# Summing the softmax exponentials of three or four query groups at once on GpSimd

## The chip, the core and the metric

The kernel runs on one core of a Trainium2 chip. The metric is the device time of one execution in microseconds; the kernel before was timed three times and its median is 1094.3 us (1091.17 to 1095.49). The profile shown below is of one more execution.

The core has four compute engines that run their own instruction streams and meet at semaphores: TensorE (PE, matmuls; PEld is its loading of weights), VectorE (DVE), ScalarE (ACT) and GpSimd (POOL). SyncE (SP) issues the transfers.

## The reference

For each of 4 batches there are 12,480 queries, keys and values of width 128, and 49 agents. All arithmetic is in float32.

```python
a2k = softmax(scale * agents @ k.T)          # 49 x 12480
agent_v = a2k @ v                            # 49 x 128
q2a = softmax(scale * q @ agents.T)          # 12480 x 49
x = q2a @ agent_v                            # 12480 x 128, all batches: 49920 rows
h = x @ w_in                                 # 49920 x 2048
out = (h * cos(h)) @ w_out                   # 49920 x 128
```

Each softmax is `e = exp(s - max)`, divided by `e.sum() + 1e-09`. The change touches how the sums `e.sum()` of `q2a` are formed: for each query, 49 exponentials are added up.

## The kernel before

**Tiling.** The queries are worked in groups of 960, 13 groups to a batch, 52 in all. A group stands in SBUF as 8 tiles (`GT`) of 120 queries; some groups are laid out on 126 partitions (`QT`), so that the exponentials `e` of one group are a 126 x 8 x 49 block. A group takes 16 steps (`STEP`); the main loop runs through 832 steps and 4 more. In a step n, TensorE makes `ph`, two 128 x 480 blocks of h (`first_product`, L1119, from the weights `a` and the turned query weights `pT`), ScalarE takes the cosine (`c`, L1122), VectorE forms `r = (cos - 1) * h` (`cubic_part`, L1128), and TensorE multiplies the `r` of step n - 4 by `w_out` (`second_product`, L1144; L1140 and L1141 add the linear part). `ph` and the small blocks called `one` lie in PSUM, all other names in SBUF. There are 3 buffers of `ph`, 6 of `r` and 3 of `pT`.

**What a query group needs before its 16 steps.** Scores `q @ agents` (L169, L177), their maximum (VectorE, `mx`, L734), the subtraction (GpSimd, `e<-e,mx`, L736 and L782), the exponential (ScalarE, L791), the sum (`query_sum`, L796 to L808), 1/sum (VectorE, `query_inverse`, L810 to L814), the product of both (GpSimd, `query_weights`, `p<-e,rz`, L819), transposes on TensorE (L833), a copy out of PSUM on ScalarE (L838) and the split into `pT` on GpSimd (L843, L844).

**Bursts and pieces.** The exponential and the sine need different tables in ScalarE, so the exponentials are collected: in each batch, at its step 97 (`BURST`), one burst takes the exponentials of a piece of 7 query groups (A), of the next batch's keys (K) and of a piece of 6 query groups (B), each as one instruction. In the last batch there is only one piece, of 5 groups. The earliest five groups have a burst of their own in which VectorE forms the sums (`vector_sum`); the first three groups, in the opening, are summed one by one on GpSimd.

**A sum on GpSimd.** `query_sum` adds up one group (8 x 49 numbers in each partition) with seven additions: 24 + 24 columns, 12 + 12, 6 + 6, 3 + 3 (all into the tile `tree`, L802), then the three left and the 49th column into `rz` (L804, L805, L806). Behind the last group of a piece one more instruction adds `EPS` to the sums of the whole piece (L808). For the opening's groups and the early piece VectorE adds `EPS` (L813).

**What sets the order.** A plan maps steps to calls. `burst` plans the seven sums of piece A at steps +1, +1, +3, +3, +9, +11 and +13 behind the burst and those of piece B at +16, +18 and so on; 1/sum of A stands at +16, of B at +42. `query_weights` of group n stands 10 steps ahead of the group, its transposes 7 ahead (or the next free place). Every engine then works its list in order. `kept_behind` ties the GpSimd instructions of a call to the one traced ahead of them, so that the sums keep their place among GpSimd's other work.

Of the kernel before, what the change touches and what calls it, by code (L numbers as in the profile page):

```python
# [9 lines left out]
F32 = mybir.dt.float32  # L10
# [8 lines left out]
P = 128  # L19
# [4 lines left out]
GT = 8  # L24
# [4 lines left out]
EPS = 1e-9  # L29
# [17 lines left out]
def agent_attention_cos_ffn(ctx, tc, qT, kT, v, vk, vk_rest, agT, w_in, w_out, outT):  # L47
    nc = tc.nc
# [70 lines left out]
    @contextmanager  # L119
    def kept_behind(engines):  # L120

        traced = nc.cur_bb.bb.instructions
        start = len(traced)
        last = {}
        for i in reversed(traced):
            if i.engine in engines and i.engine not in last:
                last[i.engine] = i
            if len(last) == len(engines):
                break
        yield  # L130
        for i in list(traced[start:]):
            if i.engine in engines:
                tc.add_manual_dep(i, last[i.engine].name, mybir.DependencyInfo(mybir.DependencyClass.NoSync,
                                  mybir.DependencyReason.DATA), reason="kept_behind")
                last[i.engine] = i
# [281 lines left out]
    class First(Fast):  # L417
# [87 lines left out]
        def summed(self):  # L505
            sums = self.sb.tile([KR, P], F32, name="sums", bufs=1)
            nc.vector.tensor_copy(sums, self.po)
            yield
            pv = self.psum()[:, :KR]
            nc.tensor.matmul(pv, sums, fold, start=True, stop=True)  # L510
            yield
            nc.vector.tensor_copy(self.av, pv)
            yield
# [159 lines left out]
    with ExitStack() as pools:  # L673
        sb = pools.enter_context(tc.tile_pool(name="sb", bufs=2))
# [26 lines left out]
        PER = NG * STEP  # L701
        NQ = NB * NG
        NSTEP = NB * PER
        e_of, rz_of, closes = {}, {}, {}
        PIECES = 7

        def piece_tiles(piece):
            e = sb.tile([QT, PIECES * GT, NA], F32, name="e", bufs=3)
            rz = sb.tile([QT, PIECES * GT], F32, name="rz2", bufs=4)
            for i, k in enumerate(piece):  # L710
                e_of[k], rz_of[k] = e[:, i * GT:(i + 1) * GT], rz[:, i * GT:(i + 1) * GT]
                e_of[piece], rz_of[piece] = e[:, :len(piece) * GT], rz[:, :len(piece) * GT]
            if piece != early:
                closes[piece[-1]] = piece

        def query_parts(n, piece, wide=False, by_vector=False):
            b, g = n // NG, n % NG
            src = qT[b, :, g * GRP:(g + 1) * GRP + (QT - TT if n in plain else 0)]
            if wide:
                ps = scores_twice(sb.tile([P, 2 * 512], F32, name="xt", bufs=3)[:, :GRP], src, b, pair())  # L720
                yield
            else:
                ps = query_scores(sb, src, b, small(), n in plain).rearrange("p (h t) a -> p h t a", h=2)
                yield
            if n == piece[0]:
                piece_tiles(piece)
            e = e_of[n].rearrange("p (h t) a -> p h t a", h=2)
            if not wide:
                (nc.vector.tensor_copy if by_vector else nc.scalar.copy)(e, ps)
                ps = e  # L730
                yield
            mx = sb.tile([QT, GT], F32, name="mx2", bufs=6)
            mx = mx.rearrange("p (h t) -> p h t", h=2)
            nc.vector.reduce_max(mx, ps, axis=AX.X)  # L734
            on = nc.vector if wide else nc.gpsimd
            on.tensor_sub(e, ps, mx.unsqueeze(3).to_broadcast([QT, 2, HT, NA]))  # L736
# [56 lines left out]
        def vector_sum(n):  # L793
            nc.vector.reduce_sum(rz_of[n], e_of[n], axis=AX.X)

        def query_sum(n):  # L796

            e, rz = e_of[n], rz_of[n].unsqueeze(2)
            t = sb.tile([e.shape[0], GT, 24], F32, name="tree", bufs=1)
            src, w = e, 24  # L800
            while w > 2:
                nc.gpsimd.tensor_add(t[:, :, :w], src[:, :, :w], src[:, :, w:2 * w])  # L802
                src, w = t, w // 2
            nc.gpsimd.tensor_add(rz, t[:, :, 0:1], t[:, :, 1:2])  # L804
            nc.gpsimd.tensor_add(rz, rz, t[:, :, 2:3])  # L805
            nc.gpsimd.tensor_add(rz, rz, e[:, :, 48:49])  # L806
            if n in closes:
                nc.gpsimd.tensor_scalar_add(rz_of[closes[n]], rz_of[closes[n]], EPS)  # L808

        def query_inverse(piece):  # L810
            rz = rz_of[piece]
            if piece not in closes.values():
                nc.vector.tensor_scalar_add(rz, rz, EPS)  # L813
            nc.vector.reciprocal(rz, rz)  # L814

# [53 lines left out]
        first, early = (0, 1, 2), (3, 4, 5, 6, 7)  # L869
# [51 lines left out]
        for x in OPENING.split():  # L921
# [4 lines left out]
            else:  # L926
                name = x.rstrip("0123456789")
# [3 lines left out]
        plan, early_plan = Plan(), Plan()  # L931
        taken = set()

        def extra(n, f, *args, dense=False):


            while n in taken or (n - LAG) % NP not in ((1, 2, 3, 4, 5) if dense else (1, 3, 5)):
                n += 1
            taken.add(n)
            plan(n, f, *args)  # L940
            return n
# [5 lines left out]
        def spread_out(todo, t, end, dense=False):  # L947

            for i, lot in enumerate(todo):
                t = extra(t, *lot, dense=dense) + 1  # L950
                if i + 1 < len(todo):
                    t += max(0, (end - t) // (len(todo) - i - 1) - 1)
            return t

        sums = []

        def summed(t, n):
            for x in [x for x in sums if x[1] == t][:n]:
                sums.remove(x)
                (vector_sum if x[2] else query_sum)(x[0])  # L960

        def in_parts(f, *args):
            if f is query:
                yield from query_parts(*args)
            else:
                yield f(*args)

        def lazy_sum(n):
            with kept_behind([nc.gpsimd.engine]):
                query_sum(n)  # L970

        def burst(t, todo, by_vector=False):
            (short if by_vector else windows).add(t)
            second = 0
            for f, *args in todo:
                plan(t, f, *args)
                if f is query_exp:
                    piece, = args
                    assert t + 4 < piece[0] * STEP - 10
                    if second and 16:  # L980
                        for i, n in enumerate(piece):
                            plan(t + 16 + 2 * i, lazy_sum, n)
                    elif by_vector:
                        sums.extend((n, t, True) for n in piece)
                    else:
                        for i, n in zip((1, 1, 3, 3, 9, 11, 13), piece):
                            plan(t + i, lazy_sum, n)
                    plan(t + (16, 42)[second], query_inverse, piece)
                    second = 1

        def scored(piece, *how):
            return [(query, n, piece, *how) for n in piece]
# [47 lines left out]
        t = spread_out(scored(early), 0, 0) + 2  # L1040
        t += (LAG + 1 - t) % NP
        burst(t, [(query_exp, early)], True)
        early_fill(t, [(ab[1].scores, g, True) for g in range(3)])
        t += 6

        def mixed(x, y):

            out, nx, ny = [], len(x), len(y)
            x, y = list(x), list(y)
            while x or y:  # L1050
                z = x if not y or x and len(x) * ny >= len(y) * nx else y
                out.append(z.pop(0))
            return out
# [4 lines left out]
        for b in range(1, NB):  # L1058
# [5 lines left out]
            t = spread_out(mixed(ks, qs[:before]), t, at - TURN, True)  # L1064
            t = extra(t, ab[b].across, dense=True)
            plan(t - 1, ab[b].top)
            t = extra(t + 1, ab[b].spread, dense=True) + 1
            for g in range(NL):
                plan(t + g, ab[b].shift, g)
            t = spread_out(qs[before:], t, at - 5, True)  # L1070
            assert t < at, (t, at)
            work = dict(A=(query_exp, ps[0]), B=(query_exp, ps[1]), K=(pinned_exp, ab[b]))
            burst(at, [work[x] for x in ('A', 'K', 'B')])
            fresh = scored(pieces[b][0], False, True)
            ahead = len(fresh)
# [6 lines left out]
            t, end = at + 9, o + PER - 26  # L1082
            todo = mixed(vs, fresh)
            for i, x in enumerate(todo):
                t = extra(t, *x, dense=True) + 1
                if i + 1 < len(todo):
                    t += max(0, (end - t) // (len(todo) - i - 1) - 1)
            t = extra(t, ab[b].folded) + 1
            t = extra(t, ab[b].inverse) + 1
            i = b % 2  # L1090
            for c in range(DFF // 512):
                t = extra(t, ab[b].project, c, a[i], dense=True) + 3
# [5 lines left out]
        t = spread_out([x for piece in pieces[NB - 1] for x in scored(piece)][ahead:], t, at - 6)  # L1098
# [115 lines left out]
    with tc.If(far):  # L1214
        with ExitStack() as pools:
            sb = pools.enter_context(tc.tile_pool(name="gsb", bufs=2))
# [129 lines left out]
```

## Time and profile before

| | us |
|---|---|
| median of 3 runs | 1094.3 |
| lowest, highest | 1091.17, 1095.49 |
| the profiled execution, its own time | 1090.91 |
| its span in the trace | 1089.1 |
| PE busy | 1038.1 (95%) |
| DVE busy | 1013.8 (93%) |
| ACT busy | 950.8 (87%) |
| POOL busy | 564.8 (52%) |

The time of an execution holds 1.8 us more than the span of its trace. The engines work beside each other, so that their busy times don't add up. A wait in the trace is put down to the instruction that released it; the granted clock (PEclk) is the share of TensorE's full speed that it was given. The bursts with two pieces lie near 200, 457 and 713 us, that of the last batch near 960 us.

### The profile page before, as it was taken

What the parts mean: (1) busy time and instruction counts of PE and PEld (TensorE: products, weight loads), DVE (VectorE), ACT (ScalarE), POOL (GpSimd) and SP (SyncE); (2) the same over time, 40 slices, a digit from 0 to 9 for tenths busy, and PEclk for the clock granted to TensorE, in tenths of its full rate; (3) what the DMA queues carried; (4) which work ended last, traced back from release to release, by engine and by line L of the source; (5) the groups of instructions that cost most, each with busy time, mean ns of one, the idle gap of its engine ahead of it and who ended that gap; (6) DMA issues with size and microseconds to landing.
All of it is one profiled execution on the core that took longest, in us unless ns stands there. A gap on an engine that the chain in (4) does not pass through costs nothing.

```text
span 1089.1 us, 27572 instructions
## 1 busy us (share of the span) xinstructions
PE 1038.1 (95%) x11325; PEld 804.2 (74%) x11325; DVE 1013.8 (93%) x1098; ACT 950.8 (87%) x1191; POOL 564.8 (52%) x870
## 2 busy tenths in 40 slices
PE   6989999889999999989999999988999999989997
PEld 2867877777878887767787888767777777767775
DVE  6879989989999999989999999988999999999997
ACT  3669888979889998888989999897989999999996
POOL 2434876785533775777533566668462322253220
PEclk9899999999999999999999999999999999999999
DMA  9933555512202334441200334442100000000001
GB/s 349 351 94 116 157 182 190 207 39 96 80 20 76 112 117 155 137 163 59 100 38 29 123 96 159 131 149 77 61 19 38 18 37 19 37 19 37 19 37 40
DMA packets 32551, 108.45 MB, mean 100 GB/s; under 512 B 3616, under 2 KB 4896, under 8 KB 32416
## 3 DMA queue, kind: packets, MB, share of 16 engines
q1 hardware_dynamic: 32416, 106.59, 29.0%
q8 instruction: 91, 1.49, 0.6%
q14 instruction: 44, 0.36, 0.1%
HBM read 81.02 MB, written 25.56 MB: 98 GB/s over the span
## 4 chain that ended last, share of the span: by engine, by line
PE 60%; DVE 18%; POOL 12%; ACT 4%; issue 4%; DMA 1%; SPq 0%; POOLq 0%; ACTq 0%; DVEq 0%
PE ph L1119 24%; PE one L1144 22%; DVE r L1128 16%; POOL tree L802 5%; PE one L560 2%; PE one L524 2%; POOL s L604 2%; ACT c L1122 2%; PE one L169 2%; PE one L1140 1%; PE one L833 1%; PE one L1141 1%; POOL pT L844 1%; PE one L381 1%; POOL e L736 1%
## 5 line engine op out<-in xcount | busy, mean ns | idle before, releaser
L1128 DVE SCALAR_TENSOR_TENSOR r<-c,ph 128x960 fp32r<-128x960 f32 x832 | 908.8, 1149 | 37.4 <-ACT c L1122 34.8
L1122 ACT ACTIVATE c<-ph 128x960 f32<-128x960 f32 x832 | 788.9, 980 | 95.1 <-PE ph L1119 71.2
L1119 PE MATMUL ph<-pT,a 113*128 113x480 f32 x1664 | 533.0, 401 | 20.4 <-DVE r L1128 14.8
L1144 PE MATMUL one<-r,w 128*128 128x480 f32 x1664 | 503.2, 389 | 0.4 <-DVE r L1128 0.4
L1119 PEld LDWEIGHTS ph<-pT,a 113*128 113x128 f32 x1664 | 290.4, 190 | 132.8 <-DVE r L1128 67.7
L1144 PEld LDWEIGHTS one<-r,w 128*128 128x128 f32 x1664 | 308.6, 190 | 50.4 <-DVE r L1128 1.4
L819 POOL TENSOR_TENSOR p<-e,rz 126x392 f32<-126x392 f32 (+1 forms) x52 | 44.2, 851 | 188.5 <-PE one L833 181.4
L844 POOL TENSOR_TENSOR pT<-p,pT 49x480 fp32r<-49x480 f32 x104 | 127.1, 1222 | 7.9
L843 POOL CAST pT<-p 49x480 fp32r<-49x480 f32 x104 | 60.7, 584 | 56.0 <-ACT p L838 51.9
L736 POOL TENSOR_TENSOR e<-e,mx 126x392 f32<-126x392 f32 x43 | 36.1, 844 | 63.5 <-DVE mx L734 63.1
L802 POOL TENSOR_TENSOR tree<-tree 126x96 f32<-126x96 f32 (+1 forms) x141 | 43.6, 309 | 10.6
L1151 ACT COPY osb<-one 128x480 f32<-128x480 f32 x80 | 44.7, 559 | 2.3 <-PE one L1144 2.2
L604 POOL TENSOR_TENSOR s<-s,mxb 128x392 f32<-128x392 f32 (+1 forms) x39 | 34.3, 916 | 17.9 <-DVE mxb L600 17.9
L577 POOL TENSOR_TENSOR over<-s,run 128x392 f32<-128x392 f32 x27 | 28.0, 1037 | 26.9 <-ACT s L564 26.7
L524 PEld LDWEIGHTS one<-s,vt 128*32 128x32 f32 (+2 forms) x2160 | 30.5, 113 | 13.8 <-issue 10.1
L560 PEld LDWEIGHTS one<-ag,xt 128*32 128x32 f32 x2340 | 28.4, 110 | 16.2 <-issue 10.7
L1140 PE MATMUL one<-pT,b 113*128 113x480 f32 x104 | 39.9, 383 | 0.0
L1141 PE MATMUL one<-pT,b 113*128 113x480 f32 x104 | 39.6, 381 | 0.0
L524 PE MATMUL one<-s,vt 128*32 128x49 f32 (+2 forms) x2160 | 35.5, 211 | 2.3 <-ACT e L791 0.8
L578 POOL TENSOR_SCALAR over<-over 128x392 f32<-128x392 f32 x30 | 35.6, 1188 | 2.6
L560 PE MATMUL one<-ag,xt 128*32 128x49 f32 x2340 | 34.0, 209 | 2.6 <-DVE s L564 1.9
L802 POOL TENSOR_TENSOR tree<-e 126x192 f32<-126x192 f32 (+1 forms) x47 | 29.0, 616 | 14.0 <-ACT e L791 9.1
(156 smaller groups left out, 754.0 us busy)
## 6 DMA issues: line engine op xcount, KB each, us to landing
outT<-osb SPq DMA_DIRECT2D x51, 480.0 KB, 2.7
xt<-kT SPq DMA_DIRECT2D x42, 512.0 KB, 3.8
vt<-vk SPq DMA_DIRECT2D x36, 512.0 KB, 4.5
xt<-qT SPq DMA_DIRECT2D x35, 480.0 KB, 3.7
xt<-qT SPq DMA_DIRECT2D x16, 483.0 KB, 4.0
c<-kT SPq DMA_DIRECT2D x6, 512.0 KB, 5.6
c<-vk SPq DMA_DIRECT2D x6, 512.0 KB, 6.0
xt<-vk SPq DMA_DIRECT2D x6, 512.0 KB, 6.3
```

The costliest lines, as they stand in the source:

```text
L524: mm = nc.tensor.matmul(po[rows], vt[:, x, rows], e, start=(first and x == 0), stop=(last and x + 1 == len(es)))
L560: mm = nc.tensor.matmul(ps[j * QS:(j + 1) * QS, t], xt[:, t * w + j * QS:t * w + (j + 1) * QS], ag[:, self.b, :], start=True, stop=True)
L604: nc.gpsimd.tensor_sub(s, s, self.mxb.unsqueeze(1).to_broadcast(list(s.shape)))
L802: nc.gpsimd.tensor_add(t[:, :, :w], src[:, :, :w], src[:, :, w:2 * w])
L843: nc.gpsimd.tensor_copy(pT[own, c], p[own])
L844: nc.gpsimd.tensor_sub(pT[other, c], p[own], pT[own, c].bitcast(F32))
L1119: nc.tensor.matmul(ph[:, j, :CH], ai[:, f], pTs[q % 3][:, c], start=True, stop=True)
L1122: nc.scalar.activation(cos, h, AF.Sin, bias=HALF_PI, scale=1.0)
L1128: nc.vector.scalar_tensor_tensor(r, cos, 1.0, h, op0=ALU.subtract, op1=ALU.mult)
L1140: nc.tensor.matmul(po, b1[k], pTs[q % 3][:, c], start=False, stop=False)
L1141: nc.tensor.matmul(po, b2[k], pTs[q % 3][:, c], start=False, stop=False)
L1144: nc.tensor.matmul(po, w1[:, f, :], r[:, j, :], start=(f == 0), stop=(f == NF - 1))
```

## The change

`query_sum` becomes `added_up`, which adds up whatever block of `e` it is given and adds `EPS` to that block's sums at its end. A piece is summed in two calls of `query_sums` instead of one call for each group: all but its last three groups (4, 3 or 2 groups), then the last three. For the first piece of a burst the calls stand at steps +1 and +3, for the second at +13 and +17. The tile `tree` grows from 8 x 24 to 32 x 24 numbers in each partition. For the opening's three groups `EPS` is now added on GpSimd and no longer on VectorE; the early piece stays as it was.

```diff
--- before.py
+++ after.py
@@ -701,7 +701,7 @@
         PER = NG * STEP
         NQ = NB * NG
         NSTEP = NB * PER
-        e_of, rz_of, closes = {}, {}, {}
+        e_of, rz_of = {}, {}
         PIECES = 7
 
         def piece_tiles(piece):
@@ -710,8 +710,6 @@
             for i, k in enumerate(piece):
                 e_of[k], rz_of[k] = e[:, i * GT:(i + 1) * GT], rz[:, i * GT:(i + 1) * GT]
                 e_of[piece], rz_of[piece] = e[:, :len(piece) * GT], rz[:, :len(piece) * GT]
-            if piece != early:
-                closes[piece[-1]] = piece
 
         def query_parts(n, piece, wide=False, by_vector=False):
             b, g = n // NG, n % NG
@@ -793,10 +791,10 @@
         def vector_sum(n):
             nc.vector.reduce_sum(rz_of[n], e_of[n], axis=AX.X)
 
-        def query_sum(n):
-
-            e, rz = e_of[n], rz_of[n].unsqueeze(2)
-            t = sb.tile([e.shape[0], GT, 24], F32, name="tree", bufs=1)
+        def added_up(e, rz):
+
+            rz = rz.unsqueeze(2)
+            t = sb.tile([P, 4 * GT, 24], F32, name="tree", bufs=1)[:e.shape[0], :e.shape[1]]
             src, w = e, 24
             while w > 2:
                 nc.gpsimd.tensor_add(t[:, :, :w], src[:, :, :w], src[:, :, w:2 * w])
@@ -804,12 +802,19 @@
             nc.gpsimd.tensor_add(rz, t[:, :, 0:1], t[:, :, 1:2])
             nc.gpsimd.tensor_add(rz, rz, t[:, :, 2:3])
             nc.gpsimd.tensor_add(rz, rz, e[:, :, 48:49])
-            if n in closes:
-                nc.gpsimd.tensor_scalar_add(rz_of[closes[n]], rz_of[closes[n]], EPS)
+            nc.gpsimd.tensor_scalar_add(rz, rz, EPS)
+
+        def query_sum(n):
+            added_up(e_of[n], rz_of[n])
+
+        def query_sums(piece, lo, hi):
+            part = slice(lo * GT, hi * GT)
+            with kept_behind([nc.gpsimd.engine]):
+                added_up(e_of[piece][:, part], rz_of[piece][:, part])
 
         def query_inverse(piece):
             rz = rz_of[piece]
-            if piece not in closes.values():
+            if piece == early:
                 nc.vector.tensor_scalar_add(rz, rz, EPS)
             nc.vector.reciprocal(rz, rz)
 
@@ -957,17 +962,13 @@
         def summed(t, n):
             for x in [x for x in sums if x[1] == t][:n]:
                 sums.remove(x)
-                (vector_sum if x[2] else query_sum)(x[0])
+                vector_sum(x[0])
 
         def in_parts(f, *args):
             if f is query:
                 yield from query_parts(*args)
             else:
                 yield f(*args)
-
-        def lazy_sum(n):
-            with kept_behind([nc.gpsimd.engine]):
-                query_sum(n)
 
         def burst(t, todo, by_vector=False):
             (short if by_vector else windows).add(t)
@@ -977,14 +978,12 @@
                 if f is query_exp:
                     piece, = args
                     assert t + 4 < piece[0] * STEP - 10
-                    if second and 16:
-                        for i, n in enumerate(piece):
-                            plan(t + 16 + 2 * i, lazy_sum, n)
-                    elif by_vector:
-                        sums.extend((n, t, True) for n in piece)
+                    if by_vector:
+                        sums.extend((n, t) for n in piece)
                     else:
-                        for i, n in zip((1, 1, 3, 3, 9, 11, 13), piece):
-                            plan(t + i, lazy_sum, n)
+                        n = len(piece)
+                        plan(t + (1, 13)[second], query_sums, piece, 0, n - 3)
+                        plan(t + (3, 17)[second], query_sums, piece, n - 3, n)
                     plan(t + (16, 42)[second], query_inverse, piece)
                     second = 1
 
```

Below stand rows of GpSimd's instruction list, in order, at the two places that matter; x2 at a row's end is two alike in a row, a shape such as 126x8x12 is partitions x tiles x columns, `e` are the exponentials and `mx` the maxima, `tree` the partial sums, `rz` the sums, `p` the weights and `pT` the turned weights; `pT_99` is one of its three buffers, and `rz_1440` and `rz_2389` are the sums of the first and the second piece of the first of these bursts.

GpSimd before, from the last subtractions of the burst on: the split into `pT` and, behind it, the fifth of the first piece's seven groups.

```order
L736 TENSOR_TENSOR e<-e,mx_3118 126x392
L736 TENSOR_TENSOR e<-e,mx_3121 126x392
L736 TENSOR_TENSOR e<-e,mx_3125 126x392
L843 CAST pT_99<-p 49x480 x2
L844 TENSOR_TENSOR pT_99<-p,pT_99 49x480 x2
L802 TENSOR_TENSOR tree<-e 126x192
L802 TENSOR_TENSOR tree<-tree 126x8x12
L802 TENSOR_TENSOR tree<-tree 126x8x6
L802 TENSOR_TENSOR tree<-tree 126x8x3
L804 TENSOR_TENSOR rz_1440<-tree 126x8
L805 TENSOR_TENSOR rz_1440<-rz_1440,tree 126x8
L806 TENSOR_TENSOR rz_1440<-rz_1440,e 126x8
```

GpSimd after, from the end of the first piece's second sum to the same split into `pT` and the second piece's first sum.

```order
L804 TENSOR_TENSOR rz_1440<-rz_1440,e 126x24
L805 TENSOR_SCALAR rz_1440<-rz_1440 126x24
L734 TENSOR_TENSOR e<-e,mx_3111 126x392
L734 TENSOR_TENSOR e<-e,mx_3114 126x392
L734 TENSOR_TENSOR e<-e,mx_3118 126x392
L848 CAST pT_99<-p 49x480 x2
L849 TENSOR_TENSOR pT_99<-p,pT_99 49x480 x2
L800 TENSOR_TENSOR tree<-e 126x576
```

Before, four of the first piece's groups are summed ahead of this split and three behind it, with the piece's `EPS` (L808) behind those; after, all seven and both `EPS` stand ahead of it.

GpSimd before, at the first group of the first piece: the weights `p` stand behind three of the second piece's six sums, and a fourth sum runs on between them.

```order
L804 TENSOR_TENSOR rz_2389<-tree 126x8
L805 TENSOR_TENSOR rz_2389<-rz_2389,tree 126x8
L806 TENSOR_TENSOR rz_2389<-rz_2389,e 126x8
L819 TENSOR_TENSOR p_104<-e,rz_1440 126x2x4x49
L802 TENSOR_TENSOR tree<-e 126x192
L819 TENSOR_TENSOR p_105<-e,rz_1440 126x2x4x49
L802 TENSOR_TENSOR tree<-tree 126x8x12
```

GpSimd after, at the same weights.

```order
L804 TENSOR_TENSOR rz_2389<-rz_2389,e 126x24
L805 TENSOR_SCALAR rz_2389<-rz_2389 126x24
L824 TENSOR_TENSOR p_104<-e,rz_1440 126x2x4x49
L824 TENSOR_TENSOR p_105<-e,rz_1440 126x2x4x49
L734 TENSOR_TENSOR e<-e,mx_3455 126x392
L824 TENSOR_TENSOR p_104<-e,rz_1440 126x2x4x49
L848 CAST pT_100<-p 49x480 x2
```

The whole second piece is now summed ahead of these weights, and nothing of it stands between or behind them. The lists of TensorE, ScalarE and SyncE are the same before and after; VectorE's loses the three additions of `EPS` in the opening and is otherwise the same.

## Rows read from the trace of the kernel before

**Rows 1.** The page's first part: busy us, share of the span, instructions

```profile
PE 1038.1 (95%) x11325; PEld 804.2 (74%) x11325; DVE 1013.8 (93%) x1098; ACT 950.8 (87%) x1191; POOL 564.8 (52%) x870
```

**Rows 2.** Waits over the span: engine, line, releaser: us, times, longest

```profile
DVE rz L814 <- POOL rz L808: 6.8, 3, 2.3
...
PEld one L833 <- POOL p L819: 2.1, 3, 0.7
```

**Rows 3.** Timeline of VectorE behind the first burst: start, us, instruction [idle before]

```profile
225.06 4.34 DVE L1128 SCALAR_TENSOR_TENSOR r<-c,ph 128x960 fp32r<-128x960 f32 x4
231.66 0.50 DVE L814 RECIPROCAL rz<-rz 126x56 f32<-126x56 f32 x1 [2.26 <-POOL rz L808]
232.08 4.28 DVE L1128 SCALAR_TENSOR_TENSOR r<-c,ph 128x960 fp32r<-128x960 f32 x4
```

**Rows 4.** Timeline of TensorE, the same stretch

```profile
225.25 0.60 PE L1119 MATMUL ph<-pT,a 113*128 113x480 f32 x2
...
230.00 0.60 PE L1144 MATMUL one<-r,w 128*128 128x480 f32 x2
233.23 0.69 PE L1119 MATMUL ph<-pT,a 113*128 113x480 f32 x2 [2.64 <-DVE r L1128]
...
234.69 1.17 PE L1119 MATMUL ph<-pT,a 113*128 113x480 f32 x2
...
240.25 0.69 PE L833 MATMUL one<-ident,p 126*113 126x126 f32 x4 [0.29 <-POOL p L819]
```

**Rows 5.** Windows between transposes: busy of PE, PEld, DVE, ACT, POOL, clock, DMA

```profile
217.88:240.25 22.37, 19.45 (x201) 15.27 (x199) 19.17 (x21) 17.13 (x22) 17.41 (x49) 0.92 0.14 47
240.25:258.21 17.96, 17.95 (x200) 14.13 (x201) 16.91 (x18) 16.05 (x19) 12.49 (x29) 1.00 0.25 87
...
730.37:752.76 22.39, 19.50 (x202) 15.37 (x200) 18.76 (x21) 16.75 (x21) 17.42 (x49) 0.92 0.22 70
752.76:770.70 17.94, 17.94 (x201) 14.14 (x202) 16.94 (x18) 16.07 (x19) 11.71 (x28) 1.00 0.27 88
```

**Rows 6.** GpSimd by line and form: busy us, mean ns | idle before

```profile
L577 POOL TENSOR_TENSOR over<-s,run 128x392 f32<-128x392 f32 x27 | 28.0, 1037 | 26.9 <-ACT s L564 26.7
L802 POOL TENSOR_TENSOR tree<-e 126x192 f32<-126x192 f32 x44 | 26.6, 604 | 9.8 <-ACT e L791 9.1
L802 POOL TENSOR_TENSOR tree<-tree 126x96 f32<-126x96 f32 x44 | 17.1, 388 | 3.2
L802 POOL TENSOR_TENSOR tree<-tree 126x48 f32<-126x48 f32 x44 | 12.5, 283 | 3.2
L802 POOL TENSOR_TENSOR tree<-tree 126x24 f32<-126x24 f32 x44 | 10.3, 234 | 3.5
...
L804 POOL TENSOR_TENSOR rz<-tree 126x8 f32<-126x8 f32 x44 | 9.0, 204 | 3.4
...
L802 POOL TENSOR_TENSOR tree<-e 120x192 f32<-120x192 f32 x3 | 2.4, 796 | 4.2 <-ACT e L758 4.2
...
L651 POOL TENSOR_TENSOR es<-es 128x49 f32<-128x49 f32 x6 | 1.5, 270 | 0.2
...
L808 POOL TENSOR_SCALAR rz<-rz 126x56 f32<-126x56 f32 x3 | 1.1, 352 | 0.3
```

**Rows 7.** Timeline of GpSimd behind the first burst

```profile
203.13 0.61 POOL L802 TENSOR_TENSOR tree<-e 126x192 f32<-126x192 f32 x1 [0.46 <-ACT e L791]
...
205.67 0.61 POOL L802 TENSOR_TENSOR tree<-e 126x192 f32<-126x192 f32 x1
...
214.83 2.45 POOL L736 TENSOR_TENSOR e<-e,mx 126x392 f32<-126x392 f32 x3
219.56 1.22 POOL L843 CAST pT<-p 49x480 fp32r<-49x480 f32 x2 [2.29 <-ACT p L838]
220.86 2.51 POOL L844 TENSOR_TENSOR pT<-p,pT 49x480 fp32r<-49x480 f32 x2
```

**Rows 8.** The chain that ended last, in the opening

```profile
60.06 0.18 DVE rz L813
```

## The prediction

> **What bounds the kernel now.** I read the page's first part, then the waits, then the timelines of VectorE, TensorE and GpSimd behind one burst, and last a table of windows. TensorE is busy for 95% of the span, VectorE for 93%, GpSimd for 52% [rows 1]. So GpSimd's busy time as such is worth nothing; its work counts only where somebody waits for its result. The windows run from one group's transposes (L833) to the next group's, 16 steps each. In an ordinary one TensorE is busy for 17.95 of 17.96 us at full clock, VectorE for 16.91 [rows 5]: TensorE sets the pace, and any idle time of its own is lost for good.
>
> The first window behind a burst is different: it takes 22.37 us instead of 17.96, behind the third burst 22.39 instead of 17.94 [rows 5], and the second repeats this. The reason is in the waits: three times, 6.8 us in total, VectorE's 1/sum (L814) waited for GpSimd's last addition of the piece (L808) [rows 2]. The timeline shows the first: VectorE stood for 2.26 us, from 229.40 to 231.66, with its steps (L1128) queued behind the 1/sum [rows 3]. TensorE ran dry: its last work ended at 230.00 + 0.60 = 230.60, and it stood for 2.64 us until a `ph` buffer came free [rows 4]. Behind the stall two matmuls that otherwise take 0.60 us took 1.17 [rows 4]; the granted clock of the window is 0.92 against 1.00 [rows 5], so part of it ran at 1.2 GHz instead of 2.4. At the window's end the transposes waited 0.29 us more for `p` from GpSimd [rows 4], which stands behind sums too.
>
> **What GpSimd's sums will cost.** A sum of one group is seven instructions. Its tree takes 604, 388, 283 and 234 ns for 192, 96, 48 and 24 numbers a partition, and the last three take some 205 ns each for 8 [rows 6]: 2.12 us, with the gaps 205.67 - 203.13 = 2.54 us from one sum to the next [rows 7], so a gap is about 0.06 us. From 24 to 192 numbers the line rises by 370 / 168 = 2.2 ns a number, and an addition of 392 takes 1037 ns [rows 6], 2.17 ns a number beyond 192. Some 180 ns of each instruction are therefore paid whatever the size; that is what a larger block shares out. Along this line, as an estimate, the instructions for four groups (768, 384, 192, 96 and three of 32 numbers) take 1.85 + 1.02 + 0.60 + 0.39 + 3 x 0.25, and the `EPS` addition 0.29, less than the 0.35 that it takes for 56 numbers [rows 6]: 4.91 us, and 5.4 with eight gaps. Three groups (576, 288, 144, 72, 24) take 1.43 + 0.81 + 0.50 + 0.34 + 3 x 0.23 + 0.27 = 4.05, and 4.55 with gaps.
>
> The trace has no addition of 768 numbers and none over 32 short rows, so I bound the two sums of the first piece (9.95 us): above by 18.1, seven sums as now with one `EPS` (7 x 2.54 + 0.35), if the fixed part belonged to the rows of a block and not to the instruction; below by 5.1, two sums of 2.54, if an addition's time did not grow with its size. The rows speak against both ends: the time does grow along the line above, and one row of 49 numbers takes 270 ns (L651), and 48 numbers in eight rows 283 [rows 6]. I take the line.
>
> **What moves.** The first piece's sums start at 203.13, when the exponentials are there [rows 7]. Before, four stood ahead of the burst's last subtractions and three behind the split into `pT`. Now both calls stand ahead, with the same five subtractions of 2.45 / 3 = 0.82 us between and behind them [rows 7]: 203.13 + 9.95 + 5 x 0.82 = 217.2 us, against 214.83 + 2.45 = 217.3 before [rows 7]. So the split into `pT` starts as now, when ScalarE has delivered `p` at 219.56, and its first half is ready at 220.86 + 1.25 = 222.1 [rows 7] for the matmul seven steps behind the transposes, at 225.25 [rows 4]. The sums that VectorE waits for are there before 217; 1/sum is due at 229.40. **The wait of 2.26 us goes, with 12 us to spare.**
>
> Behind the split, at 223.4, now come both sums of the second piece: 2 x 4.55 = 9.1, until 232.5, and then the weights `p`, 0.84 more. The transposes that need them are due at about 236.2 (below), so the wait of 0.29 goes too. Queued behind `p` are only a subtraction, the next `p`, which waits for those transposes as before, and the next `pT`.
>
> **What it is worth.** In the window of the first burst TensorE is idle for 22.37 - 19.45 = 2.92 us [rows 5]. What stays: the 1/sum still takes its place in VectorE's list. Its first step behind it led to TensorE's next matmul at 233.23, 1.57 us after the 1/sum began [rows 3, 4]; from 229.40 that is 230.97, and TensorE would still stand from 230.60, 0.37 us. So 2.55 us of idle time go. The slow clock cost 19.45 - 17.95 = 1.50 us for the same work [rows 5] (201 matmuls against 200); I count it as gone, since a stall of 0.37 us is like the small ones that leave the ordinary windows at 1.00. That is 4.05 us, and the window becomes 18.3 us. Three bursts: 12.15 us. The last batch's burst has no such wait of VectorE (the three of rows 2 are the bursts with two pieces), and its two sums are shorter: nothing.
>
> TensorE's clock deserves a second look. The windows behind a burst show it lowered, to 0.92 each, and the ordinary ones do not [rows 5]. The Trainium skill ("TensorE: Matmul & The Clock Gate", What's actually happening) says that the monitor behind the clock runs freely, so that the same kernel can show different numbers of slow matmuls from run to run; the alike windows here don't show that. By that rule the 1.50 us need not come back in every execution; the sum would then be 3 x 2.55 = 7.65 us.
>
> **The opening** loses a little: three additions of `EPS` move to GpSimd, 0.25 us and a gap each, and two of them stand on the way to work that is waited for; one takes the place of VectorE's 0.18 us on the chain [rows 8]. 0.31 + 0.31 - 0.18 = 0.4 us, between -0.2 (VectorE's own additions are gone) and 0.9 (all three in the way).
>
> Sum: -12.15 + 0.4 = -11.75 us. The profiled execution took 1090.91 us, 3.4 under the median of 1094.3; the change brings it to 1079.2, and the median to **1082.5 us**.
>
> **The rivals.**
>
> *VectorE takes over the bound.* Its busy time in the window behind the burst is 19.17 us, with 18 of its steps instead of 16 [rows 5]; if all of that must pass within the window, it can't fall below 19.2 + small gaps. Then the gain is 3.0 a burst, -9 + 0.4, 1085.7. Against it: the two extra steps are a lead that it builds while TensorE stands and runs slowly; in the next window it needs only 16.91. Chance 0.08.
>
> *The clock does not come back*, because it falls for the burst's own short pauses and not for the stall: 3 x 2.55 less 0.4, 1087.1. For it, that a term of 1.50 rests on one cause in the trace; against it, that the slow matmuls begin only behind the stall [rows 4]. Chance 0.11.
>
> *The larger sums are slow*, one mechanism with two outcomes. Let them cost f times my estimate. The second piece's sums now stand ahead of `p`, all of them. `p` is ready at 219.56 (or 207.2 + 9.95 f, if that is later) + 3.9 + 9.1 f + 0.84, and due at 236.2. At f = 1.3 it is 0.5 us late, at 1.45 some 3.4 us, which is the stall that was removed, in a new place: no gain, 1094. At f = 1.6 `pT` is late by 0.4 us and `p` by 5.8 more; with 2 us of slow clock that is 8.6 against 4.4 now, 3 x 4.2 + 0.4 = 13 us slower, 1107. It decides from f = 1.5. For it: in the opening the same addition took 796 ns instead of 604 [rows 6], 1.32 times, and 18.1 / 9.95 is 1.8. Against it: behind the bursts it took its 604 beside VectorE's steps, and the rows against a price by row. The Trainium skill ("GPSIMD Engine Reference", Key points) names contention with VectorE's instructions that read two inputs from SBUF; VectorE's steps here read `c` from SBUF and `ph` from PSUM, so by that rule too f stays near 1 behind a burst. Chance 0.10 for no change, 0.07 for slower.
>
> **How the numbers follow.** The forecast has 0.64; its own range is 1079 (the profiled execution) to 1086 (the slowest of the three runs less 10). With 0.08 and 0.11 for the two smaller gains, faster by over 0.5% (5.5 us, about what a measurement of this kernel can tell from no change) has 0.83, within it 0.10, slower 0.07. The range 1078 to 1089 takes in both smaller gains and the scatter of the three runs and leaves out the last rival with its two outcomes.
>
> **What would show it.** VectorE's wait for `rz` gone from the list; the window behind a burst about 18.3 us at a clock of 1.00, TensorE idle for under 0.5 us in it; GpSimd's 768-number addition near 1.85 us, both sums of the first piece done by 215 us, a busy time of about 529 us (13 sums of 2.12 become 17.1 us in each of three batches, and 5 become 7.3). The prediction is wrong if `p` or `pT` appears among TensorE's waits, if the 576- and 768-number additions take over 1.4 times the estimate, or if the window stays above 20 us.

## The result, and the profile after

The changed kernel takes 1081.2 us in the median (1080.48 to 1081.63, 4 runs) against 1093.44 of the kernel before (4 runs): a ratio of 0.9888, 95% interval 0.9866 to 0.9910, so 12.2 us less. The profiled execution took 1081.35 us with a span of 1079.5. The changed file is one line shorter and its lines have moved, so the line numbers differ: L824 is the weights `p` (L819 before), L838 the transposes, L819 the 1/sum, L1118 and L1127 the matmul and VectorE's step.

The first part of the page:

```profile
PE 1032.7 (96%) x11325; PEld 800.3 (74%) x11325; DVE 1012.0 (94%) x1095; ACT 950.5 (88%) x1191; POOL 532.0 (49%) x670
```

The waits that answer to [rows 2]:

```profile
DVE rz L819 <- POOL rz L805: 1.8, 3, 0.7
...
PEld one L838 <- POOL p L824: 0.7, 1, 0.7
```

The three waits of up to 2.3 us are gone; the three that are left, of up to 0.7 us, belong to the three groups of the opening, and so does the one of the transposes (L838). The timeline of VectorE behind the first burst, as in [rows 3]:

```profile
227.94 4.34 DVE L1127 SCALAR_TENSOR_TENSOR r<-c,ph 128x960 fp32r<-128x960 f32 x4
232.19 0.50 DVE L819 RECIPROCAL rz<-rz 126x56 f32<-126x56 f32 x1
232.61 4.29 DVE L1127 SCALAR_TENSOR_TENSOR r<-c,ph 128x960 fp32r<-128x960 f32 x4
```

No wait stands ahead of the 1/sum. TensorE in the same stretch, as in [rows 4]:

```profile
233.76 0.69 PE L1118 MATMUL ph<-pT,a 113*128 113x480 f32 x2 [0.29 <-DVE r L1127]
...
239.02 0.59 PE L838 MATMUL one<-ident,p 126*113 126x126 f32 x4
```

It stands for 0.29 us where it stood for 2.64, and the transposes at the window's end no longer wait. The windows, as in [rows 5] (the three behind a burst, then the next one of the first):

```profile
220.76:239.02 18.26, 17.97 (x202) 14.19 (x200) 18.10 (x20) 16.80 (x21) 14.26 (x23) 1.00 0.17 57
473.09:491.37 18.28, 18.00 (x201) 14.17 (x200) 18.11 (x20) 16.80 (x21) 14.27 (x23) 1.00 0.16 56
725.16:743.25 18.09, 17.81 (x201) 14.26 (x200) 17.92 (x20) 16.33 (x20) 13.42 (x22) 1.00 0.26 86
239.02:256.85 17.83, 17.83 (x201) 14.05 (x200) 17.50 (x19) 16.08 (x19) 4.47 (x5) 1.00 0.25 88
```

18.26 us where it was 22.37, at full clock. GpSimd's additions by form, as in [rows 6]:

```profile
L800 POOL TENSOR_TENSOR tree<-e 126x576 f32<-126x576 f32 x10 | 14.5, 1454 | 0.5
L800 POOL TENSOR_TENSOR tree<-tree 126x288 f32<-126x288 f32 x10 | 8.0, 802 | 0.5
L800 POOL TENSOR_TENSOR tree<-e 126x768 f32<-126x768 f32 x3 | 5.6, 1870 | 1.5 <-ACT e L789 1.5
...
L803 POOL TENSOR_TENSOR rz<-rz,tree 126x24 f32<-126x24 f32 x10 | 2.5, 250 | 0.8
...
L805 POOL TENSOR_SCALAR rz<-rz 126x32 f32<-126x32 f32 x3 | 0.9, 295 | 0.3
```

And GpSimd's timeline behind the first burst, as in [rows 7]:

```profile
206.21 1.88 POOL L800 TENSOR_TENSOR tree<-e 126x768 f32<-126x768 f32 x1 [0.47 <-ACT e L789]
...
217.60 0.27 POOL L805 TENSOR_SCALAR rz<-rz 126x24 f32<-126x24 f32 x1
...
222.45 1.23 POOL L848 CAST pT<-p 49x480 fp32r<-49x480 f32 x2 [2.05 <-ACT p L843]
...
226.35 1.47 POOL L800 TENSOR_TENSOR tree<-e 126x576 f32<-126x576 f32 x1
...
235.76 1.65 POOL L824 TENSOR_TENSOR p<-e,rz 126x392 f32<-126x392 f32 x2
```

The first piece's sums are done 14 us ahead of the 1/sum, the second piece's in 9.4 us, and `p` is there 2.4 us ahead of its transposes (235.76 + 0.82 against 239.02).

### The profile page after: what moved, and what is told of

It reads as the page before. It is cut to its first block, busy times and chain, and to the rows that moved or that the text cites. A ratio compares the mean times of both kernels' runs of the same rounds, so it can differ in the third digit from the quotient of the medians.

```text
span 1079.5 us, 27373 instructions
## 1 busy us (share of the span) xinstructions
PE 1032.7 (96%) x11325; PEld 800.3 (74%) x11325; DVE 1012.0 (94%) x1095; ACT 950.5 (88%) x1191; POOL 532.0 (49%) x670
## 4 chain that ended last, share of the span: by engine, by line
PE 65%; DVE 20%; ACT 5%; POOL 5%; issue 3%; DMA 1%; SPq 0%; ACTq 0%; POOLq 0%; DVEq 0%
PE ph L1118 26%; PE one L1143 24%; DVE r L1127 19%; PE one L524 3%; PE one L560 2%; ACT c L1121 2%; POOL s L604 2%; PE one L169 2%; PE one L1139 2%; PE one L838 1%; PE one L1140 1%; PE one L381 1%; ACT s L607 1%; PE ph L502 1%; POOL tree L800 1%
## 5 line engine op out<-in xcount | busy, mean ns | idle before, releaser
L1127 DVE SCALAR_TENSOR_TENSOR r<-c,ph 128x960 fp32r<-128x960 f32 x832 | 908.1, 1150 | 32.4 <-ACT c L1121 29.6
L1118 PE MATMUL ph<-pT,a 113*128 113x480 f32 x1664 | 530.5, 400 | 13.1 <-DVE r L1127 7.6
L1118 PEld LDWEIGHTS ph<-pT,a 113*128 113x128 f32 x1664 | 288.8, 189 | 125.4 <-DVE r L1127 60.7
L824 POOL TENSOR_TENSOR p<-e,rz 126x392 f32<-126x392 f32 (+1 forms) x52 | 44.3, 856 | 221.2 <-PE one L838 211.7
L613 POOL TENSOR_TENSOR es<-es,s 128x392 f32<-128x392 f32 (+1 forms) x33 | 32.3, 980 | 2.6
L169 PEld LDWEIGHTS one<-ag,xt 128*32 128x32 f32 (+1 forms) x2112 | 25.1, 109 | 11.4 <-issue 7.9
```

Source lines behind the costliest of these rows:

```text
L169: mm = nc.tensor.matmul(out[at:at + n], xt[:, t * TT + lo:t * TT + lo + n], ag, start=True, stop=True)
L1118: nc.tensor.matmul(ph[:, j, :CH], ai[:, f], pTs[q % 3][:, c], start=True, stop=True)
L1127: nc.vector.scalar_tensor_tensor(r, cos, 1.0, h, op0=ALU.subtract, op1=ALU.mult)
```

## The experiments

**Only the wait taken away.** In the kernel before, 1/sum is planned later; the sums stay single.

```diff
-plan(t + (16, 42)[second], query_inverse, piece)
+plan(t + (16 if by_vector else 20, 42)[second], query_inverse, piece)
```

> The kernel before, with VectorE's 1/sum of the first piece planned 4 steps later (step +20 for +16), so that its sums are there in time; GpSimd's sums stay as they were, one group at a time. Theory that the removed wait alone makes the gain: the window behind a burst falls from 22.4 to about 18.3 us and the time to some 1083 us. Theory that GpSimd's list is a second limit in the same window (its work ran without a pause from 203 to 240 us and the weights p came at 240.2): VectorE's wait goes, but the transposes of the next group, then due at 236.2, wait some 4 us for p; the window stays at 22 to 23 us and the time within 3 us of before.

Measured: 1099.1 us (1097.61 to 1100.84) against 1092.44, ratio 1.0059, interval 1.0037 to 1.0080: slower. TensorE in the window behind the first burst and at the end of the third's; then the first burst's window and the one that follows it, and the ones that follow the windows of the second and the third burst:

```profile
237.61 0.71 PE L1119 MATMUL ph<-pT,a 113*128 113x480 f32 x2 [0.47 <-DVE r L1128]
242.03 0.90 PE L833 MATMUL one<-ident,p 126*113 126x126 f32 x4 [3.71 <-POOL p L819]
...
758.54 1.14 PE L833 MATMUL one<-ident,p 120*113 120x120 f32 x4 [4.08 <-POOL p L819]
```

```profile
219.60:242.03 22.43, 18.25 (x201) 13.86 (x199) 20.81 (x22) 17.71 (x22) 17.46 (x49) 1.00 0.12 48
242.03:261.51 19.48, 19.48 (x201) 15.49 (x202) 15.04 (x16) 15.32 (x18) 12.50 (x29) 0.91 0.25 80
...
499.88:520.20 20.32, 20.27 (x201) 16.35 (x202) 15.21 (x16) 15.41 (x18) 12.49 (x29) 0.87 0.22 78
...
758.54:779.18 20.64, 20.60 (x200) 16.62 (x201) 15.20 (x16) 15.43 (x18) 11.69 (x28) 0.85 0.25 76
```

VectorE's wait is gone and nothing is gained: the transposes wait 3.71 us for `p` (3.71 and 4.08 behind the two other bursts), the window is as long as before, and the slow clock falls into the next window, which takes 19.48 us for 17.96. The later 1/sum is not what holds `p` back: it starts at 235.58 and `p` at 241.13, with GpSimd's sums back to back in between, and `p` comes 21.5 us behind the window's start as it did before. So there were two limits in one place, and the second showed 0.29 us in the trace because the first hid the rest. (GpSimd's work did pause once in the stretch that the expectation names, for 2.29 us ahead of 219.56 [rows 7]; from there to `p` it ran through.) That the time would stay within 3 us of before was wrong by the slow windows, which take 19.5 to 20.6 us behind the three bursts.

**Both limits taken away by order alone.** The same, and the second piece's sums planned behind `p`. GpSimd does all it did before.

```diff
-plan(t + 16 + 2 * i, lazy_sum, n)
+plan(t + 24 + 2 * i, lazy_sum, n)
```

> The kernel before with its single sums, VectorE's 1/sum of the first piece at step +20 and the six sums of the second piece from step +24 on for +16, which puts them behind the weights p. Nothing is made smaller. Theory that what counts is only when the 1/sum and p are ready, not GpSimd's work: p is ready at 235 us for transposes due at 236.2, the window falls to 18.3 to 18.8 us and the time to 1081 to 1084 us. Rival, that fewer instructions on GpSimd are themselves worth time: 1088 or more.

Measured: 1080.93 us (1080.31 to 1081.78), ratio 0.9891, interval 0.9869 to 0.9914: the whole gain. The page, the window, and GpSimd's `p`, which now follows the 1/sum:

```profile
PE 1032.2 (96%) x11325; PEld 799.8 (74%) x11325; DVE 1012.8 (94%) x1098; ACT 950.0 (88%) x1191; POOL 566.1 (52%) x870
```

```profile
218.40:236.93 18.53, 18.06 (x201) 14.04 (x200) 18.20 (x20) 16.73 (x21) 12.22 (x29) 1.00 0.17 58
```

```profile
235.02 1.65 POOL L819 TENSOR_TENSOR p<-e,rz 126x392 f32<-126x392 f32 x2 [2.84 <-DVE rz L814]
```

GpSimd is busy for 566 us as before, and the time is that of the changed kernel. The 33 us that the change saves on GpSimd are worth nothing as such, as far as the scatter lets one see: this version keeps `EPS` of the opening on VectorE, and beside the last one below, which does so too and has the larger sums, it is 0.6 us behind.

**The place without the size.** The changed kernel, with a call for each group at the new steps.

```diff
-plan(t + (1, 13)[second], query_sums, piece, 0, n - 3)
-plan(t + (3, 17)[second], query_sums, piece, n - 3, n)
+for i in range(n):
+    plan(t + ((1, 13) if i < n - 3 else (3, 17))[second], query_sums, piece, i, i + 1)
```

> The changed kernel, with one call for each single group (eight instructions each) at the new steps: the place of the change without its size. Theory (a sum of one group with EPS takes 2.85 us, so seven take 20 us ahead of the split into pT and six take 17 us ahead of p): pT is some 4.5 us late and p some 8 us more, the window behind a burst takes 31 to 35 us, and the time is 1120 to 1130 us. Rival, that the place makes the gain and the size nothing: 1081 us.

Measured: 1131.68 us, ratio 1.0350, interval 1.0326 to 1.0375, 1.7 us above the range that was expected. TensorE's two waits behind the first burst, and the window:

```profile
232.50 1.17 PE L1118 MATMUL ph<-pT,a 113*128 113x480 f32 x2 [4.85 <-POOL pT L849]
252.63 1.18 PE L838 MATMUL one<-ident,p 126*113 126x126 f32 x4 [6.86 <-POOL p L824]
```

```profile
220.12:252.63 32.51, 20.62 (x201) 15.77 (x200) 21.11 (x22) 17.68 (x22) 26.71 (x79) 0.82 0.10 32
```

This is the rival of the slow sums, forced: `pT` is late by 4.85 us (4.5 expected) and `p` by 6.86 (8 expected), at the two places that it named.

**The size without the place.** The changed kernel, its calls at the old steps.

```diff
-plan(t + (1, 13)[second], query_sums, piece, 0, n - 3)
-plan(t + (3, 17)[second], query_sums, piece, n - 3, n)
+plan(t + (1, 16)[second], query_sums, piece, 0, n - 3)
+plan(t + (9, 22)[second], query_sums, piece, n - 3, n)
```

> The changed kernel, with the two calls of a piece at the steps where the kernel before had its first sums and those behind the split: +1 and +9 for the first piece, +16 and +22 for the second: the size of the change without its place. Theory: the first piece's sums end 1 us ahead of VectorE's 1/sum, p stands behind two sums as in the changed kernel; the window stays at 18.3 us and the time within 2 us of the changed kernel (1081). Rival, that the place is what counts: VectorE waits again, 1090 or more.

Measured: 1081.34 us (1078.30 to 1084.09), ratio 0.9894, interval 0.9862 to 0.9927; the window:

```profile
220.42:238.69 18.27, 17.98 (x202) 14.16 (x200) 18.10 (x20) 16.78 (x21) 15.01 (x24) 1.00 0.17 58
```

With sums this short the two sets of steps give the same time. What the old steps use up is slack: the first piece's sums now end at 230.64, 1.2 us ahead of the 1/sum at 231.87, where the new steps leave 14. How much later they could stand was not tried.

**The wait put back in three sizes.** In the changed kernel the `EPS` addition of the first piece's last three groups is moved behind the second piece's first sum, with idle additions ahead of it that lengthen the wait. The part of the edit that matters (the lines that plan this call are left out):

```diff
+def closed_late(piece, lo, hi):
+    rz = rz_of[piece][:, lo * GT:hi * GT]
+    with kept_behind([nc.gpsimd.engine]):
+        for k in (4,):           # (4, 2) and (4, 4) in the two others
+            e = e_of[piece][:, :k * GT]
+            t = sb.tile([P, 4 * GT, 24], F32, name="tree", bufs=1)[:e.shape[0], :e.shape[1]]
+            nc.gpsimd.tensor_add(t, e[:, :, :24], e[:, :, 24:48])
+        nc.gpsimd.tensor_scalar_add(rz, rz, EPS)
```

> The changed kernel, with the EPS addition of the first piece's last three groups moved behind the second piece's first sum, and one idle addition of 768 numbers (its result is not used) ahead of it, so that VectorE's 1/sum waits some 1.1 us behind each of the three bursts; nothing else waits. Theory that the stall itself brings the slow clock: the window behind a burst is 18.3 + 1.1 = 19.4 us, with up to 1 us of slow clock. Rival, that the clock fell in the kernel before for another reason: 19.4 us at a granted clock of 1.00. Time 1084.5 to 1088.

> As e7_wait_1, with a further idle addition of 384 numbers: VectorE's 1/sum waits some 2.2 us, the length of the wait that the change removed, with no other part of the change undone. Theory: TensorE stands some 2.5 us, the granted clock of the window falls to 0.92 as before, the window takes 22 to 22.4 us and the time is that of the kernel before, 1092 to 1093.5. Rival, that the clock fell for another reason: the window takes 20.5 us at a clock of 1.00 and the time is 1088.

> As e7_wait_1, with two idle additions of 768 numbers: VectorE's 1/sum waits some 3.1 us. Theory: TensorE stands 3.4 us, the clock falls for as long or longer than in the kernel before, the window takes 23 to 24 us and the time is 1095 to 1098. Rival, that the clock fell for another reason: 21.4 us at a clock of 1.00, 1090.5.

Measured, with VectorE's wait, TensorE's stall and the window behind the first burst of each (the windows of the two other bursts repeat these within 0.3 us). One idle addition, 1084.74 us, ratio 0.9922 (0.9893 to 0.9952):

```profile
DVE rz L829 <- POOL rz L823: 3.0, 3, 1.0
```

```profile
234.61 0.70 PE L1131 MATMUL ph<-pT,a 113*128 113x480 f32 x2 [1.40 <-DVE r L1140]
```

```profile
220.49:239.86 19.37, 17.97 (x201) 14.18 (x200) 18.17 (x20) 16.80 (x21) 15.97 (x25) 1.00 0.14 54
```

Two, of 768 and 384 numbers, 1091.23 us, ratio 0.9983 (0.9965 to 1.0000):

```profile
DVE rz L829 <- POOL rz L823: 6.3, 3, 2.1
```

```profile
235.54 0.71 PE L1131 MATMUL ph<-pT,a 113*128 113x480 f32 x2 [2.47 <-DVE r L1140]
...
237.42 1.17 PE L1131 MATMUL ph<-pT,a 113*128 113x480 f32 x2
```

```profile
220.35:242.14 21.79, 19.32 (x202) 15.58 (x201) 18.67 (x20) 16.92 (x21) 17.30 (x26) 0.92 0.14 48
```

Two of 768, 1094.58 us, ratio 1.0023 (1.0008 to 1.0037):

```profile
DVE rz L829 <- POOL rz L823: 8.7, 3, 2.9
```

```profile
236.65 0.70 PE L1131 MATMUL ph<-pT,a 113*128 113x480 f32 x2 [3.27 <-DVE r L1140]
```

```profile
220.65:243.22 22.57, 19.30 (x202) 15.55 (x200) 18.65 (x20) 16.90 (x21) 18.11 (x26) 0.92 0.14 46
```

A wait of 1.0 us costs 1.1 us of window and no clock: TensorE stood for 19.37 - 17.97 = 1.40 us. A window at a clock of 1.00 is also what the rival expected of this run, so that by itself it decides nothing. A wait of 2.1 costs 3.5: TensorE stood for 2.47, and its work took 1.35 us more at a clock of 0.92, as two matmuls behind the stall show with 1.17 us for some 0.6. A wait of 2.9 costs 4.3, with 1.33 of slow clock. Both come out a little under what was expected, 0.2 and 0.4 us in the window and 0.8 and 0.4 us in the time. The same 0.92 stands in all three windows of both kernels, six of six, and in none of the three with the short wait. So the 1.5 us of slow clock in the kernel before came from the stall, which the rival excludes, and a wait of the old length alone brings the time back to within 2 us of before.

**The opening put back.** The changed kernel with `EPS` of the first three groups on VectorE.

```diff
-            nc.gpsimd.tensor_scalar_add(rz, rz, EPS)
+            if eps:
+                nc.gpsimd.tensor_scalar_add(rz, rz, EPS)
...
-            added_up(e_of[n], rz_of[n])
+            added_up(e_of[n], rz_of[n], False)
...
-            if piece == early:
+            if piece == early or piece in first:
```

> The changed kernel with EPS of the opening's three groups on VectorE again, as before; the pieces' sums stay as changed. Theory (the step of the prediction): the move in the opening cost 0.4 us, so this is 0.4 us faster than the changed kernel, 1080.8, which is within the scatter. Rival: the opening of the changed kernel's profile ended 2.9 us later than that of the kernel before because of this move; then 1078 to 1079 us and an opening that ends near 217.9 us.

Measured: 1080.32 us (1079.11 to 1081.11), ratio 0.9886, interval 0.9865 to 0.9906; beside the changed kernel's 0.9888 that is not to be told from nothing. The traces tell more. The first matmul of the main loop, in the changed kernel and here:

```profile
65.34 0.67 PE L1118 MATMUL ph<-pT,a 113*128 113x480 f32 x2 [0.55 <-DVE a L384]
```

```profile
63.26 0.67 PE L1119 MATMUL ph<-pT,a 113*128 113x480 f32 x2 [0.55 <-DVE a L384]
```

All six profiled executions with `EPS` on GpSimd start it between 64.79 and 65.37 us, all four with `EPS` on VectorE between 62.40 and 64.27: means of 65.15 and 63.14. At the transposes behind the first burst the difference is still 1.8 us (means of 220.47 and 218.69). Of the 2.9 us by which the changed kernel's profile is later there than that of the kernel before, this version gives back 1.9 (218.88 for 220.76); the expectation's 217.9 is not reached. In the times of the runs 0.9 us of it is seen between the medians, and 0.2 us between the ratios, each against the kernel before that was measured beside it; both are within the scatter. This version, the changed kernel, the one by order alone and the one by size alone, with ratios of 0.9886 to 0.9894, can't be told apart by their times.

## Why the prediction was right

**The wait of VectorE** was the right place, and it went with 14 us to spare (12 forecast). What the step does not say is that its removal is worth something only together with the next one: without that, the kernel gets slower (1.0059).

**The weights `p`.** The prediction had them ready by 233.3 for transposes due at 236.2, and counted the end of their wait at 0.29 us. The profile after is 2.9 us later at this place, and less those 2.9 us both moments came as forecast, `p` within 0.4 us (236.6) and the transposes within 0.1 (239.02). What the step did not say is how much hung on it: 3.71 us, hidden in the trace of before by the wait ahead of it.

**The cost of the sums.** Additions of 768 and 576 numbers were put at 1.85 and 1.43 us and took 1.87 and 1.45; the sums of the first piece 9.95 and took 10.0 (217.87 - 206.21 less two subtractions of 0.82), those of the second 9.1 and took 9.4. The line through the smaller sizes held to twice the largest, and no price by row appeared. GpSimd is busy for 532 us, forecast 529. The bound of 18.1 for the first piece's sums was not touched.

**The window.** 18.3 us forecast, 18.26 measured; 0.37 us of idle time forecast to stay, 0.29 measured. The clock's 1.50 us came back, and the three sizes of wait show why: it falls with the stall. The three windows together gave 22.37 - 18.26, 22.42 - 18.28 and 22.39 - 18.09, 12.6 us (12.15 forecast); the one of the second burst before was

```profile
474.20:496.62 22.42, 19.49 (x202) 15.34 (x200) 19.17 (x21) 17.25 (x22) 17.45 (x49) 0.92 0.14 46
```

The prediction left it open whether the 1.50 us would come back in every execution. In the four kernels without a long stall here (the changed one, order alone, size without place, the shortest wait) the clock is 1.00 in all twelve windows behind the bursts; one execution of each was profiled.

**The opening** was mis-sized. It was put at 0.4 us, between -0.2 and 0.9; the first matmul comes 2.0 us later. The step counted the instructions' own time and left out what stands behind them, as far as the traces show it. They show GpSimd's last part of the first `pT` at 1.52 us in all six executions with `EPS` on GpSimd and at 1.25 in the four others, and TensorE's wait behind it at 2.68 to 3.76 us against 2.03 to 3.00. The two overlapping ranges of that wait differ by 0.9 us in their means, less than half of the 2.0. Why that addition to `pT` takes longer was not tried, and where the rest comes from stays open.

**The sum.** -11.75 forecast, -12.2 measured against the four runs of before, -11.6 against the 22 runs beside the last experiments (median 1092.79). That the sum came out so close has some luck in it: by the traces the windows gave 0.4 us more than forecast and the opening took more than forecast, so that the two errors are opposed. The two profiled executions are only 9.6 us apart (1090.91 and 1081.35): 12.6 us less in the windows, and a start of the first window that is 2.9 us later, of which 1.8 is the mean difference named above.

**The rivals.** VectorE did not take over: the window holds 18.10 us of its work in 18.26, down from 19.17, and TensorE's 17.97 fill it as well. The slow sums did not come, and the experiment that forces them shows their two waits at the places named; there the sums take about twice the estimate and the kernel loses 39 us. The clock's rival is refuted twice: the same bursts stand in the changed kernel at a clock of 1.00, and the waits put back bring the slow clock back.

## What to carry to other kernels

A wait that the trace shows may hide a longer one a little later on the same path: follow the list of the late engine on to its next result that somebody waits for, and compare both with the times at which they would be due without the first wait. Then the cheapest cure can be an order, not less work: here two planned steps gave the same 1.1% as the larger blocks. Larger blocks give slack instead, since they share out the fixed part of each instruction; both placings that were tried for them took the same time.

## What the runs showed of the hardware

In the windows behind the bursts a stall of TensorE of 1.36 to 1.40 us was followed by no fall of the granted clock (three of three), and one of 2.46 to 3.30 us by a clock of 0.92 over the window (nine of nine), part of it at 1.2 GHz instead of 2.4. There the slow clock cost 1.3 to 1.6 us and no more behind the longer of these stalls. The price is no constant, though: in the run with only the wait taken away, stalls of 3.71, 3.71 and 4.08 us were followed by windows in which TensorE's work took 1.5, 2.3 and 2.7 us more than in the kernel before (19.48, 20.27 and 20.60 us for 17.94 to 17.98).

Behind the bursts an addition on GpSimd of 24 to 768 numbers a partition goes along one line, about 180 ns and 2.2 ns a number, whether they lie in 1, 8 or 32 rows (234 ns for 24, 604 for 192, 1454 for 576, 1870 for 768). In the opening the addition of 192 numbers took 0.60 to 0.95 us; why, no run here shows.
